# Query products of two tiles at a time in quarters of TensorE's array, normalized into SBUF, with fewer PSUM banks for the attention

## The chip, the cores and the metric

The kernel runs on one core of a Trainium2 chip. The metric is the device time of one execution in microseconds. All data are float32.

## The reference

The kernel fuses a linear attention with a feed-forward layer. What is computed:

```python
kv  = np.einsum('bhsd,bhse->bhde', k, v)          # 8 batches, 8 heads, 576 positions, 64 wide
out = np.einsum('bhsd,bhde->bhse', q, kv)
rms = np.sqrt(np.mean(out * out, axis=-1, keepdims=True) + 1e-06)
out = out / rms * g_norm                          # per head
x   = out.transpose(0, 2, 1, 3).reshape(4608, 512)
h   = x @ w_in                                    # 512 -> 2048
r   = np.maximum(h, 0.0)
y   = (r * r) @ w_out                             # 2048 -> 512
```

In the attention each head's keys-values matrix `kv` is 64 by 64, and each query row is multiplied by the matrix of its own head.

## The kernel before

The 4608 rows are cut into 36 tiles of 128 rows, and four tiles make a strip. Nine strips pass through the feed-forward layer one after the other. Up and down projections of most strips are done with a scheme of seven products instead of eight (Strassen's kind): `up` runs products 1, 2, 6, 5, 7, 3, 4 (`ORDER`) for each of four column groups, and `down` or `down_deep` does the same for the way down. The products accumulate in four PSUM banks called `ps_A` (two buffers), `ps_B` and `ps_C`. ScalarE copies some of them to SBUF (`snap`, L573), VectorE adds others and applies the squared relu (L622, L623). A product of `up` is eight records on TensorE, "a step" below.

The attention of the next strip is cut into small pieces (`slices`) that `attend` puts between the steps of the strip at hand, so the attention's matmuls stand in TensorE's queue among those of the feed-forward layer. Their order is written out by hand; no planner moves them. All engines take their instructions in the order in which they were recorded. The pieces, for batch `b` and pair of heads `p`:

- `transposed_query` (L320): queries transposed so that two heads of 64 lie on 128 partitions. For the first two batches TensorE does it, through PSUM; later VectorE does.
- `key_value` (L344): ten matmuls, each giving 64 rows of output from 64 columns, so that the two heads stand side by side in the two column halves of the array. ScalarE copies the two 64 by 64 results onto the diagonal of a 128 by 128 matrix `kvd`, whose other half is zero (L353, L354).
- `query(n)` (L411): `products_x` multiplies one tile's transposed queries by `kvd`, four matmuls of 128 by 128 by 128 (L380). Every ninth tile, made of the remaining 64 rows of two batches, takes eight matmuls with 64 columns of weights (L375). Then ScalarE squares the tile (L386), VectorE sums by head (L388), and after a square root and a Newton step (L389 to L400) VectorE multiplies by the inverse norm (L407). For later tiles this product is written back into the PSUM bank.
- `features` (L454, on TensorE, tiles 4 to 8) or `squares_x` (L462, for tiles 9 to 35: VectorE transposes blocks of 32 by 32, a DMA on SP's queue writes to DRAM, and four more read back) lay the tile out as the feed-forward layer's input `xT`.

The first four tiles have code of their own (`first_queries`, `first_normalized`, `first_features`), used in the first 30 us.

All PSUM tiles of the attention share four banks of the pool `apsum`, under the tag `at`. With the four of the feed-forward layer these are all eight.

Of the kernel before, what the change touches and what calls it, by code (L numbers as in the profile page):

```python
# [10 lines left out]
FP32 = mybir.dt.float32  # L11
# [3 lines left out]
AF = mybir.ActivationFunctionType  # L15
ALU = mybir.AluOpType
AX = mybir.AxisListType
# [3 lines left out]
def kernel(  # L21
# [34 lines left out]
    nc = tc.nc  # L56
    P = 128
    B, H, S, D = q.shape
    n_tok = B * S
    d_model = H * D  # L60
    d_ff = moe_w_in.shape[1]
    NP = H // 2
    FC = d_ff // P
    C = S // P
    REST = S - C * P
    PAIR = 2 * C + 1
    assert 2 * REST == P
    N_TILE = n_tok // P
    NT = 4
# [6 lines left out]
    X_ON_PE = 2  # L76
# [3 lines left out]
    qkv_pool = ctx.enter_context(tc.tile_pool(name="qkv", bufs=2))  # L80
    rest_pool = ctx.enter_context(tc.tile_pool(name="rest", bufs=1))
    qt_pool = ctx.enter_context(tc.tile_pool(name="qt", bufs=NP + 1))
    xn_pool = ctx.enter_context(tc.tile_pool(name="xn", bufs=2))
    xt_pool = ctx.enter_context(tc.tile_pool(name="xt", bufs=2))
    small = ctx.enter_context(tc.tile_pool(name="small", bufs=3))
    g_pool = ctx.enter_context(tc.tile_pool(name="g", bufs=4))
# [1 line left out]
    conv = ExitStack()  # L88
    raw_pool = conv.enter_context(tc.tile_pool(name="raw", bufs=8))
    wtmp = conv.enter_context(tc.tile_pool(name="wtmp", bufs=4))  # L90
    apsum = ctx.enter_context(tc.tile_pool(name="apsum", bufs=4, space=bass.MemoryType.PSUM))
    fpsum = ctx.enter_context(tc.tile_pool(name="fpsum", bufs=1, space=bass.MemoryType.PSUM))
    ctx.enter_context(tc.manual_schedule())

# [68 lines left out]
    def load_next(q_eng=nc.sync):  # L163
        u = next(to_load, None)
        if u is not None:
            load(*u, q_eng)
# [144 lines left out]
    qT, kvd, x_n, xt = {}, {}, {}, {}  # L311
    flat = lambda t: t.rearrange("p h d -> p (h d)")

    def open_rest(b):
        t = qt_pool.tile([P, NP, P], FP32, name="qT_rest", tag="qT_rest", bufs=1)
        for p in range(NP):
            qT["rest", b // 2, p] = t[:, p]
        return t

    def transposed_query(b, p):  # L320
        t = main.pop(("q", b, p))
        if b >= Q_ON_PE:
            qT[b, p] = qt_pool.tile([P, C, P], FP32, name="qT", tag="qT")
            nc.vector.transpose(out=flat(qT[b, p]), in_=flat(t))
            if b % 2 and p == NP - 1:
                nc.vector.transpose(
                    out=open_rest(b).rearrange("p q (k t) -> p q k t", k=4),
                    in_=squares(q_rest[b // 2]).rearrange("p k q f -> p q k f"),
                )
            return  # L330
        ps = apsum.tile([P, C, P], FP32, name="t_ps", tag="at")
        for c in range(C):
            nc.tensor.transpose(ps[:, c, :], flat(t[:, c]), ident)
        qT[b, p] = qt_pool.tile([P, C, P], FP32, name="qT", tag="qT")
        nc.scalar.copy(qT[b, p], ps)
        if b % 2:
            t = q_rest[b // 2][:, 2 * p : 2 * p + 2]
            ps = apsum.tile([P, P], FP32, name="tr_ps", tag="at")
            nc.tensor.transpose(ps, flat(t), ident)
            if p == 0:  # L340
                open_rest(b)
            nc.scalar.copy(qT["rest", b // 2, p], ps)

    def key_value(b, p):  # L344
        tk, tv = main.pop(("k", b, p)), main.pop(("v", b, p))

        ps = apsum.tile([P, D], FP32, name="kv_ps", tag="at")
        for c in range(C + 1):
            for h in range(2):
                a, w = (tk[:, h, c, :], tv[:, h, c, :]) if c < C else (k_rest[:, 2 * p + h], v_rest[:, b % 2, 2 * p + h])  # L350
                nc.tensor.matmul(ps[ts(h, D)], lhsT=a, rhs=w, start=c == 0, stop=c == C)  # L351
        d = kv_all[:, (NP * b + p) % (2 * NP + 1)]
        nc.scalar.copy(d[0:D, 0:D], ps[0:D])  # L353
        nc.scalar.copy(d[D:P, D:P], ps[D:P])  # L354
        kvd[b, p] = d
        if b < 2:
            if b == 1 and p < 2:
                load_next()
        else:
            load_next()  # L360
            if p == NP - 1 and b + 1 < B:
                load_rest(b + 1, nc.sync)
                load_q_rest(b + 1, nc.sync)

    by_head = lambda t: t.rearrange("p (h d) -> p h d", d=D)

    def products_x(n):
        m, c = divmod(n, PAIR)
        ps = apsum.tile([P, d_model], FP32, name="x_ps", tag="at")
        for p in range(NP):  # L370
            o = ps[:, ts(p, P)]
            if c == C:
                for h in range(2):
                    half = slice(REST * h, REST * (h + 1))
                    nc.tensor.matmul(  # L375
                        o[half], lhsT=qT["rest", m, p][:, half], rhs=kvd[2 * m + h, p], start=True, stop=True
                    )
            else:
                b, c_b = (2 * m, c) if c < C else (2 * m + 1, c - C - 1)
                nc.tensor.matmul(o, lhsT=qT[b, p][:, c_b, :], rhs=kvd[b, p], start=True, stop=True)  # L380
        return ps

    def mean_squares(ps):
        n = ps.shape[-1] // D
        sq = xn_pool.tile([P, d_model], FP32, name="sq", tag="sq", bufs=1)
        nc.scalar.activation(sq, ps, AF.Square)  # L386
        ms = small.tile([P, H], FP32, name="ms", tag="ms")
        nc.vector.reduce_sum(out=ms, in_=by_head(sq), axis=AX.X)  # L388
        nc.vector.tensor_scalar(out=ms, in0=ms, scalar1=1.0 / D, scalar2=EPS, op0=ALU.mult, op1=ALU.add)  # L389
        return ms  # L390

    def inverse_root(ms):
        r = small.tile([P, H], FP32, name="rms", tag="rms")
        nc.scalar.activation(r, ms, AF.Sqrt)
        nc.vector.reciprocal(r, r)

        t = small.tile([P, H], FP32, name="newton", tag="newton")
        nc.vector.scalar_tensor_tensor(out=t, in0=ms, scalar=-0.5, in1=r, op0=ALU.mult, op1=ALU.mult)
        nc.vector.tensor_tensor(out=t, in0=t, in1=r, op=ALU.mult)
        nc.vector.scalar_tensor_tensor(out=r, in0=t, scalar=1.5, in1=r, op0=ALU.add, op1=ALU.mult)  # L400
        return r

    def normalized(n, ps, r):

        on_pe = n < X_ON_PE * C + (X_ON_PE > 1)
        x_n[n] = xn_pool.tile([P, d_model], FP32, name="x_n", tag="x_n") if on_pe else ps
        nc.vector.tensor_tensor(  # L407
            out=by_head(x_n[n]), in0=by_head(ps), in1=r.unsqueeze(2).to_broadcast([P, H, D]), op=ALU.mult
        )

    def query(n):  # L411
        ps = products_x(n)
        normalized(n, ps, inverse_root(mean_squares(ps)))

    first = {}

    def first_queries(p):
        ps = apsum.tile([P, NT, P], FP32, name="x_ps", tag="at")  # L420
        for n in range(NT):
            nc.tensor.matmul(ps[:, n, :], lhsT=qT[0, p][:, n, :], rhs=kvd[0, p], start=True, stop=True)
        first[p] = flat(ps), mean_squares(flat(ps))

    def first_normalized(p):
        ps, ms = first.pop(p)
        x_n["first", p] = t = xn_pool.tile([P, NT, P], FP32, name="x_n", tag="x_n")
        r = inverse_root(ms)
        nc.vector.tensor_tensor(
            out=by_head(flat(t)), in0=by_head(ps), in1=r.unsqueeze(2).to_broadcast([P, H, D]), op=ALU.mult  # L430
        )
# [9 lines left out]

    def first_features(p):
        t, x = x_n.pop(("first", p)), open_xt(0)
        ps = apsum.tile([P, NT, P], FP32, name="xt_ps", tag="at")
        for n in range(NT):
            nc.tensor.transpose(ps[:, n, :], t[:, n, :], ident)
        nc.scalar.activation(x[:, :, p, :], flat(ps).rearrange("p (a t) -> p a t", t=SQ), AF.Copy, scale=g_col)

    def open_xt(s):
        if s not in xt:  # L450
            xt[s] = xt_pool.tile([P, STRIP // SQ, NP, SQ], FP32, name="xT", tag="xT")
        return xt[s]
# [40 lines left out]
    slices, ready = [], {}  # L493
# [10 lines left out]
    for b in range(1, B):  # L504
        for p in range(NP):
            slices += [(transposed_query, (b, p)), (key_value, (b, p))]
        first_n = b // 2 * PAIR + (C if b % 2 else 0)
        ns = list(range(first_n, first_n + C + b % 2))
        for i in range(len(ns) + 1):
            if i < len(ns):  # L510
                slices.append((query, (ns[i],)))
            if 0 < i <= len(ns):
                slices.append((features if b < X_ON_PE else squares_x, (ns[i - 1],)))
            if i > 0 and ns[i - 1] % NT == NT - 1:
                ready[ns[i - 1] // NT] = len(slices)
    slice_at = [0]

    def attend(n):
# [216 lines left out]
    place = lambda s, p: LAST_PLACE if s == N_STRIP - 1 and p in (5, 3) else PLACE  # L735
# [170 lines left out]
```

## Time and profile before

| What | Value |
|---|---|
| Median of 7 runs | 949.74 us (948.86 to 954.33) |
| The profiled execution | 950.99 us, its span 949.2 us |
| TensorE matmuls busy | 923.0 us, 97% |
| TensorE weight loads busy | 817.6 us, 86% |
| VectorE busy | 671.1 us, 71% |
| ScalarE busy | 231.2 us, 24% |
| DMA, mean over the span | 196 GB/s |
| Granted TensorE clock | 0.998 |

The profile counts a float32 matmul of the products as two records, each with its own weight load: the 112 matmuls of L380 are 224 records. A record lasts longer than the distance to the next one, because matmuls overlap in the array. What a matmul costs is therefore read from the distance between starts in the timeline and not from its mean duration.

### The profile page before, as it was taken

How to read it: one execution, taken by the hardware profiler on the slowest of the kernel's cores; microseconds unless marked ns; L12 is line 12 of the kernel's file. 1: busy time of each engine (PE TensorE's matmuls, PEld its weight loads, DVE VectorE, ACT ScalarE, POOL GpSimd, SP SyncE). 2: the span in 40 equal slices, each digit the busy share in tenths (PEclk: the TensorE clock that was granted, in tenths of full speed). 3: DMA queues.
4: the chain of work that ended last, by engine and by line, in shares of the span. 5: the costliest groups of instructions: out<-in, count | busy, mean ns of one | idle time of the engine just before them, and what ended most of it. 6: DMA issues, size and time to landing. Idle time of an engine off the chain costs nothing.

```text
span 949.2 us, 15646 instructions
## 1 busy us (share of the span) xinstructions
PE 923.0 (97%) x6144; PEld 817.6 (86%) x6144; DVE 671.1 (71%) x1217; ACT 231.2 (24%) x508; POOL 1.7 (0%) x7
## 2 busy tenths in 40 slices
PE   4899999999999999999999999999999999999998
PEld 3444888888888998899989998999889988998898
DVE  3998864585447995589648974798569854983396
ACT  3797441320023102210222012201220022002200
POOL 0000000000000000000000000000000000000000
PEclk9999999999999999999999999999999999999999
DMA  8799884536984586548663875387516821692075
GB/s 249 254 298 294 268 231 144 123 113 225 314 245 121 202 299 187 118 159 308 210 146 99 307 248 135 92 292 244 170 29 244 286 88 63 213 310 70 0 254 179
DMA packets 164281, 185.85 MB, mean 196 GB/s; under 512 B 83952, under 2 KB 137712, under 8 KB 155632
## 3 DMA queue, kind: packets, MB, share of 16 engines
q1 hardware_dynamic: 163888, 184.72, 61.6%
q8 instruction: 48, 0.79, 0.3%
q10 hardware_dynamic: 320, 0.13, 0.1%
q14 instruction: 25, 0.20, 0.1%
HBM read 153.62 MB, written 31.20 MB: 195 GB/s over the span
## 4 chain that ended last, share of the span: by engine, by line
PE 90%; DVE 4%; DMA 4%; ACT 1%; issue 1%; SPq 0%; DVEq 0%; ACTq 0%
PE ps_A L563 29%; PE ps_B L748 18%; PE ps_A L748 14%; PE ps_B L563 14%; PE ps_C L563 7%; PE x_ps L380 3%; PE kv_ps L351 2%; DMA raw<-in_moe_w_out_dram 2%; PE ps_A L599 1%; DMA w_blk<-w_out 1%; PE ps_B L599 1%; DVE w_c L222 1%; DMA q_rest<-in_q_dram 1%; DMA q<-in_q_dram 0%; PE x_ps L375 0%
## 5 line engine op out<-in xcount | busy, mean ns | idle before, releaser
L563 PE MATMUL ps_A<-x_t,w_in 128*128 128x256 f32 x768 | 182.6, 381 | 1.3 <-DVE gt L622 1.3
L563 PEld LDWEIGHTS ps_A<-x_t,w_in 128*128 128x128 f32 x768 | 143.6, 190 | 21.1 <-DVE gt L622 2.1
L748 PE MATMUL ps_B<-w_blk,g_s 128*128 128x128 f32 x896 | 109.2, 275 | 0.0
L748 PEld LDWEIGHTS ps_B<-w_blk,g_s 128*128 128x128 f32 x896 | 104.6, 192 | 0.0
L748 PE MATMUL ps_B<-w_blk,gt 128*128 128x128 f32 x672 | 84.2, 275 | 0.0
L748 PE MATMUL ps_A<-w_blk,g_s 128*128 128x128 f32 x672 | 81.9, 275 | 0.0
L748 PEld LDWEIGHTS ps_B<-w_blk,gt 128*128 128x128 f32 x672 | 80.1, 192 | 0.4
L748 PEld LDWEIGHTS ps_A<-w_blk,g_s 128*128 128x128 f32 x672 | 78.4, 192 | 0.0
L622 DVE TENSOR_TENSOR gt<-ps_C,snap 128x512 f32<-128x512 f32 x32 | 22.1, 690 | 66.8 <-PE ps_C L563 66.7
L623 DVE SCALAR_TENSOR_TENSOR gt<-gt 128x512 f32<-128x512 f32 x96 | 66.5, 692 | 3.3
L573 ACT COPY snap<-ps_A 128x512 f32<-128x512 f32 x68 | 39.8, 586 | 113.7 <-PE ps_A L563 101.3
L622 DVE TENSOR_TENSOR gt<-ps_A,snap 128x512 f32<-128x512 f32 x32 | 22.0, 688 | 61.6 <-PE ps_A L563 61.5
L748 PE MATMUL ps_A<-w_blk,gt 128*128 128x128 f32 x504 | 63.1, 275 | 0.0
L563 PE MATMUL ps_A<-xT,w_in 128*128 128x256 f32 x256 | 61.2, 382 | 0.0
L563 PE MATMUL ps_C<-xT,w_in 128*128 128x256 f32 x256 | 61.0, 381 | 0.0
L242 DVE TENSOR_TENSOR gt<-gt 128x2048 f32<-128x2048 f32 (+1 forms) x31 | 58.1, 1874 | 4.0 <-PE ps_C L563 3.8
L563 PE MATMUL ps_B<-x_t,w_in 128*128 128x256 f32 x256 | 60.9, 381 | 0.0
L563 PE MATMUL ps_B<-xT,w_in 128*128 128x256 f32 x256 | 60.7, 380 | 0.0
L748 PEld LDWEIGHTS ps_A<-w_blk,gt 128*128 128x128 f32 x504 | 59.7, 192 | 0.0
L388 DVE TENSOR_REDUCE ms<-sq 128x8 f32<-128x512 f32 x36 | 24.6, 684 | 44.9 <-ACT sq L386 44.2
L563 PEld LDWEIGHTS ps_C<-xT,w_in 128*128 128x128 f32 x256 | 48.1, 190 | 6.8 <-issue 0.2
L563 PEld LDWEIGHTS ps_B<-xT,w_in 128*128 128x128 f32 x256 | 48.3, 190 | 6.5
(117 smaller groups left out, 1236.0 us busy)
## 6 DMA issues: line engine op xcount, KB each, us to landing
w_blk<-w_deep SPq DMA_DIRECT2D x49, 1024.0 KB, 5.5
w_blk<-w_out SPq DMA_DIRECT2D x49, 768.0 KB, 5.2
w_blk<-w_out SPq DMA_DIRECT2D x11, 1024.0 KB, 6.5
raw<-in_moe_w_in_dram SPq DMA_DIRECT2D x16, 512.0 KB, 6.4
raw<-in_moe_w_out_dram SPq DMA_DIRECT2D x16, 512.0 KB, 6.2
k<-in_k_dram SPq DMA_DIRECT2D x30, 256.0 KB, 2.9
v<-in_v_dram SPq DMA_DIRECT2D x30, 256.0 KB, 3.3
w_deep<-w_t SPq DMA_DIRECT2D x7, 1024.0 KB, 8.6
```

Source lines behind the costliest of these rows:

```text
L222: yield nc.vector.scalar_tensor_tensor(out=ci, in0=high, scalar=-(2**30), in1=ci, op0=ALU.bitwise_and, op1=ALU.bitwise_or)
L242: eng.tensor_tensor(out=out, in0=a, in1=b, op=ALU.subtract)
L351: nc.tensor.matmul(ps[ts(h, D)], lhsT=a, rhs=w, start=c == 0, stop=c == C)
L380: nc.tensor.matmul(o, lhsT=qT[b, p][:, c_b, :], rhs=kvd[b, p], start=True, stop=True)
L388: nc.vector.reduce_sum(out=ms, in_=by_head(sq), axis=AX.X)
L563: nc.tensor.matmul(bank[BANK[p]][:, i, :], lhsT=lhsT(k), rhs=rhs(k), start=p in (1, 5, 2) and i == 0 and k == 0, stop=k == n - 1, skip_gro ...
L573: nc.scalar.copy(snap[p], b)
L599: nc.tensor.matmul(ps, lhsT=w_in[:, kc % KH, g, kc // KH * 2 + fh, ts(i, P)], rhs=xt[0][:, :, kc, :], start=kc == 0, stop=kc == NP - 1,)
L622: nc.vector.tensor_tensor(out=o, in0=b, in1=a, op=ALU.add)
L623: nc.vector.scalar_tensor_tensor(out=o, in0=o, scalar=0.0, in1=o, op0=ALU.max, op1=ALU.mult)
L748: nc.tensor.matmul(chain[c][x][:, i, :], lhsT=a[:, f, :], rhs=w[:, f, :], start=p not in (6, 7, 3) and j in ((1, 2) if place(s, p) is LAST ...
```

## The change

`products_x` now takes one or two tiles. Each matmul of 128 by 128 by 128 becomes four of 64 by 64 by 64: the contraction is cut by head (`row`, the two row halves of the array), and the output rows by 64 (`half`, the two column halves). The zero halves of `kvd` are no longer read. The two row halves write to different PSUM banks: the output is one tile of two banks, with the tag `x` and one buffer, indexed by row half, then tile, then column. The ninth tiles are done in the same way and may share a call with their neighbour.

The tiles of a batch are taken by twos: (query, query, normalize, features or squares for each). A batch with an odd number has five tiles, hence two pairs and a single; one with an even number has four, hence two pairs. Batches 1 to 7 make 14 pairs and 4 singles. `query` holds the matmuls, the squares and the sums, and `normalized`, a piece of its own, holds the square root, the Newton step (now once for both tiles) and the multiplication. This writes to SBUF (`x_n`) for all tiles, and puts the heads back in order on the way. The pool `xn` has three buffers shared by `sq`, `x_n` and `x_q`; before it had two and one for `sq` alone.

`apsum` keeps two banks for `at`. The transposed queries of batches 0 and 1 use the two-bank tile `x`; the transposes of the remaining rows use the free columns of the bank that the keys-values product will use. The first four tiles use the banks `A`, `B` and `C` of the feed-forward layer, which is not running yet.

```diff
-    xn_pool = ctx.enter_context(tc.tile_pool(name="xn", bufs=2))
+    xn_pool = ctx.enter_context(tc.tile_pool(name="xn", bufs=3))
...
-    apsum = ctx.enter_context(tc.tile_pool(name="apsum", bufs=4, space=bass.MemoryType.PSUM))
+    apsum = ctx.enter_context(tc.tile_pool(name="apsum", bufs=2, space=bass.MemoryType.PSUM))
...
-        ps = apsum.tile([P, C, P], FP32, name="t_ps", tag="at")
+        ps = apsum.tile([P, 2, C, P], FP32, name="t_ps", tag="x", bufs=1)[:, 0]
...
-            ps = apsum.tile([P, P], FP32, name="tr_ps", tag="at")
+            kv_places[b, p] = apsum.tile([P, 2 * P], FP32, name="kv_ps", tag="at")
+            ps = kv_places[b, p][:, P : 2 * P]
...
-        ps = apsum.tile([P, D], FP32, name="kv_ps", tag="at")
+        place = kv_places.pop((b, p), None) or apsum.tile([P, 2 * P], FP32, name="kv_ps", tag="at")
+        ps = place[:, 0:D]
...
-    def products_x(n):
-        m, c = divmod(n, PAIR)
-        ps = apsum.tile([P, d_model], FP32, name="x_ps", tag="at")
+    def products_x(ns):
+
+        ps = apsum.tile([P, 2, 2, d_model // 2], FP32, name="x_ps", tag="x", bufs=1)
         for p in range(NP):
-            o = ps[:, ts(p, P)]
-            if c == C:
+            for i, n in enumerate(ns):
+                m, c = divmod(n, PAIR)
                 for h in range(2):
                     half = slice(REST * h, REST * (h + 1))
...
-                b, c_b = (2 * m, c) if c < C else (2 * m + 1, c - C - 1)
-                nc.tensor.matmul(o, lhsT=qT[b, p][:, c_b, :], rhs=kvd[b, p], start=True, stop=True)
+                    if c == C:
+                        q, b = qT["rest", m, p], 2 * m + h
+                    else:
+                        b, c_b = (2 * m, c) if c < C else (2 * m + 1, c - C - 1)
+                        q = qT[b, p][:, c_b]
+                    for r in range(2):
+                        row = slice(D * r, D * (r + 1))
+                        nc.tensor.matmul(
+                            ps[half, r, i, ts(p, D)], lhsT=q[row, half], rhs=kvd[b, p][row, row], start=True, stop=True
+                        )
         return ps
...
+    def mean_squares(parts):
+        ms = small.tile([P, 2, H], FP32, name="ms", tag="ms")[:, : len(parts)]
+        for i, ps in enumerate(parts):
+            sq = xn_pool.tile(list(ps.shape), FP32, name="sq", tag="x_n")
+            nc.scalar.activation(sq, ps, AF.Square)
...
+    def query(ns):
+        ps = products_x(ns)
+        parts = [ps[:, :, i] for i in range(len(ns))]
+        queried.append((parts, mean_squares(parts)))
+
+    def normalized(ns):
+        parts, ms = queried.pop()
+        r = inverse_root(ms)
+        for i, n in enumerate(ns):
+            x_n[n] = xn_pool.tile([P, d_model], FP32, name="x_n", tag="x_n")
+            o = x_n[n].rearrange("p (q r d) -> p r q d", r=2, d=D)
+            x = parts[i].rearrange("p r (q d) -> p r q d", d=D)
+            w = r[:, i].rearrange("p (r q) -> p r q", r=2).unsqueeze(3).to_broadcast([P, 2, NP, D])
+            nc.vector.tensor_tensor(out=o, in0=x, in1=w, op=ALU.mult)
...
-        ps = apsum.tile([P, NT, P], FP32, name="x_ps", tag="at")
+        ps = fpsum.tile([P, NT, P], FP32, name="x_ps", tag="A", bufs=2)
...
-        ps = apsum.tile([P, NT, P], FP32, name="xt_ps", tag="at")
+        ps = fpsum.tile([P, NT, P], FP32, name="xt_ps", tag="BC"[p % 2])
...
-        for i in range(len(ns) + 1):
-            if i < len(ns):
-                slices.append((query, (ns[i],)))
-            if 0 < i <= len(ns):
-                slices.append((features if b < X_ON_PE else squares_x, (ns[i - 1],)))
-            if i > 0 and ns[i - 1] % NT == NT - 1:
-                ready[ns[i - 1] // NT] = len(slices)
+        for i in range(0, len(ns), 2):
+            slices += [(query, (ns[i : i + 2],)), (normalized, (ns[i : i + 2],))]
+            for n in ns[i : i + 2]:
+                slices.append((features if b < X_ON_PE else squares_x, (n,)))
+                if n % NT == NT - 1:
+                    ready[n // NT] = len(slices)
```

More of the change, by code (lines that the diff above doesn't have):

```diff
@@ L318, in open_rest @@
         return t
+    kv_places = {}
     def transposed_query(b, p):
@@ L365 @@
     by_head = lambda t: t.rearrange("p (h d) -> p h d", d=D)
-    def products_x(n):
-        m, c = divmod(n, PAIR)
-        ps = apsum.tile([P, d_model], FP32, name="x_ps", tag="at")
+    def products_x(ns):
+        ps = apsum.tile([P, 2, 2, d_model // 2], FP32, name="x_ps", tag="x", bufs=1)
         for p in range(NP):
-            o = ps[:, ts(p, P)]
-            if c == C:
+            for i, n in enumerate(ns):
+                m, c = divmod(n, PAIR)
                 for h in range(2):
                     half = slice(REST * h, REST * (h + 1))
[L375 to L378, printed above, removed]
-                b, c_b = (2 * m, c) if c < C else (2 * m + 1, c - C - 1)
-                nc.tensor.matmul(o, lhsT=qT[b, p][:, c_b, :], rhs=kvd[b, p], start=True, stop=True)
-        return ps
[L383 to L388, printed above, removed]
+                    if c == C:
[8 more added lines that the diff above has]
+                        )
+        return ps
+    def mean_squares(parts):
[3 more added lines that the diff above has]
+            nc.scalar.activation(sq, ps, AF.Square)
+            if len(ps.shape) == 3:
+                sq = sq.rearrange("p r e -> p (r e)")
+            nc.vector.reduce_sum(out=ms[:, i], in_=by_head(sq), axis=AX.X)
         nc.vector.tensor_scalar(out=ms, in0=ms, scalar1=1.0 / D, scalar2=EPS, op0=ALU.mult, op1=ALU.add)
@@ L392, in inverse_root @@
     def inverse_root(ms):
-        r = small.tile([P, H], FP32, name="rms", tag="rms")
+        r, t = (small.tile([P, 2, H], FP32, name=n, tag=n)[:, : ms.shape[1]] for n in ("rms", "newton"))
         nc.scalar.activation(r, ms, AF.Sqrt)
         nc.vector.reciprocal(r, r)
-        t = small.tile([P, H], FP32, name="newton", tag="newton")
         nc.vector.scalar_tensor_tensor(out=t, in0=ms, scalar=-0.5, in1=r, op0=ALU.mult, op1=ALU.mult)
@@ L401, in inverse_root @@
         return r
[L403 to L413, printed above, removed]
+    queried = []
+    def query(ns):
[11 more added lines that the diff above has]
+            nc.vector.tensor_tensor(out=o, in0=x, in1=w, op=ALU.mult)
     first = {}
     def first_queries(p):
-        ps = apsum.tile([P, NT, P], FP32, name="x_ps", tag="at")
+        ps = fpsum.tile([P, NT, P], FP32, name="x_ps", tag="A", bufs=2)
         for n in range(NT):
             nc.tensor.matmul(ps[:, n, :], lhsT=qT[0, p][:, n, :], rhs=kvd[0, p], start=True, stop=True)
-        first[p] = flat(ps), mean_squares(flat(ps))
+        first[p] = flat(ps), mean_squares([flat(ps)])
     def first_normalized(p):
@@ L427, in first_normalized @@
         x_n["first", p] = t = xn_pool.tile([P, NT, P], FP32, name="x_n", tag="x_n")
-        r = inverse_root(ms)
+        r = inverse_root(ms)[:, 0]
         nc.vector.tensor_tensor(
```

## The prediction

> **What bounds the kernel now.** I read the page first, its busy times and the row of slices, then the groups of instructions kept apart by shape, then the timeline of TensorE where query products stand.
>
> ```profile
> PE 923.0 (97%) x6144; PEld 817.6 (86%) x6144; DVE 671.1 (71%) x1217; ACT 231.2 (24%) x508; POOL 1.7 (0%) x7
> PE   4899999999999999999999999999999999999998
> PEclk9999999999999999999999999999999999999999
> ```
>
> TensorE (PE) is full from about 75 us to the end, at full clock. Every microsecond taken out of its queue after about 100 us should shorten the span, as long as nothing else is late. All query products but those of the first four tiles lie there:
>
> ```profile
> L380 PE MATMUL x_ps<-kv_all,qT 128*128 128x128 f32 x224 | 29.5, 275 | 0.0
> L375 PE MATMUL x_ps<-kv_all,qT_rest 128*64 128x128 f32 x64 | 4.8, 280 | 0.9 <-ACT kv_all L354 0.9
> L351 PE MATMUL kv_ps<-v,k 128*64 128x64 f32 x480 | 21.4, 234 | 0.0
> L388 DVE TENSOR_REDUCE ms<-sq 128x8 f32<-128x512 f32 x36 | 24.6, 684 | 44.9 <-ACT sq L386 44.2
> L407 DVE TENSOR_TENSOR x_ps<-x_ps,rms 128x512 f32<-128x512 f32 x27 | 18.9, 700 | 3.2 <-DVE rms L400 0.5
> ```
>
> L380 waits for nothing: what it costs is its length. The price is the distance between starts (first column, us):
>
> ```profile
> 501.84 1.89 PE L563 MATMUL ps_C<-xT,w_in 128*128 128x256 f32 x8
> 503.56 1.05 PE L380 MATMUL x_ps<-kv_all,qT 128*128 128x128 f32 x8
> 504.45 1.89 PE L563 MATMUL ps_A<-x_t,w_in 128*128 128x256 f32 x8
> 506.18 1.89 PE L563 MATMUL ps_B<-x_t,w_in 128*128 128x256 f32 x8
> ```
>
> A step of `up` takes 506.18 - 504.45 = 1.73 us, and a tile of L380 takes 504.45 - 503.56 = 0.89 us. Now a stretch with both kinds of half-array work:
>
> ```profile
> 688.62 0.81 PE L563 MATMUL ps_A<-x_t,w_in 128*128 128x256 f32 x3
> 689.37 0.69 PE L351 MATMUL kv_ps<-v,k 128*64 128x64 f32 x16
> 689.88 0.29 PE L351 MATMUL kv_ps<-v_rest,k_rest 128*64 128x64 f32 x4
> 690.10 1.99 PE L563 MATMUL ps_B<-x_t,w_in 128*128 128x256 f32 x8
> 691.93 1.89 PE L563 MATMUL ps_A<-x_t,w_in 128*128 128x256 f32 x8
> ...
> 696.21 1.99 PE L563 MATMUL ps_A<-x_t,w_in 128*128 128x256 f32 x8
> 698.13 1.09 PE L375 MATMUL x_ps<-kv_all,qT_rest 128*64 128x128 f32 x16
> 699.15 1.99 PE L563 MATMUL ps_A<-xT,w_in 128*128 128x256 f32 x8
> 700.99 0.38 PE L563 MATMUL ps_C<-xT,w_in 128*128 128x256 f32 x1
> ```
>
> The sixteen records of L351 start within 0.51 us, though each lasts 222 ns. Record by record in the same trace they start in twos, one for each column half, 7 ns apart, and a new two follows every 58.4 ns. **So the halves of the array do work side by side.** Entering and leaving this mode costs: three L563 records (0.216 each) from 688.62 end at 689.27, but L351 starts at 689.37 (0.10); its first two stand 0.05 longer than the later ones; the last is followed by L563 0.09 late; and the next step takes 1.83 instead of 1.73 (0.10). Together 0.34 us a block.
>
> **PE: what goes.** 28 tiles of L380 at 0.893 us: 25.0. Four tiles of L375: a start 0.09 late (1.92 after the step before, where a step behind keys-values takes 1.83), 1.02 long, next step 0.11 longer: 1.22 each, 4.9. Sum 29.9 us.
>
> **PE: what comes.** A tile is 16 matmuls of 64 by 64 by 64, 32 records, four to a set with one in each quarter. If all four run side by side as the two of L351 do, a set takes 58.4 ns: the stream is as long (64 columns) and so is the weight load. A pair is 16 sets, 0.93, and with the change of mode 1.28 us; a single is 0.47 + 0.34 = 0.81. 14 x 1.28 + 4 x 0.81 = 21.2 us. **Gain 8.7 us.** The changed order of instructions has 18 such blocks, each between two whole steps, so the change of mode is paid once for each.
>
> No row of before shows work in two row halves, so the set's time is the uncertain term. From below it is 58.4 ns (one stream's own time). From above it is twice that, if row halves take turns (a pair then 2.21 us). I take the lower end: the nearest row is L351, which differs only in its rows.
>
> **A rule against it.** The Trainium skill's page "TensorE: Matmul & The Clock Gate", section "Back-to-back issue gap", gives about 60 cycles (some 25 ns) as the least distance between starts for 1 to 64 columns. By it four records cost 100 ns and not 58.4, a pair 1.95 and all blocks 14 x 1.95 + 4 x 1.15 = 31.9 us: an estimate of 2 us lost. The row says otherwise for different tiles of the array: 7 ns between the two of L351, hence four in about 28 ns, below 58.4. I take the row. But L351 has only 20 records, which may have been queued ahead; a pair has 64. Semaphore records of PE's sequencer show how fast it fills the queue: at 12.75, 12.89 and 13.01 us it passed four matmuls each in about 0.13 us with the semaphore's own 0.05, some 20 ns a matmul, and a quarter matmul (two records) is needed only every 29 ns. So supply should hold.
>
> **Waits and the other engines.** ScalarE's squares and VectorE's sums, multiplications and block transposes stay, one each a tile at the same sizes (0.60, 0.68, 0.70, 0.71 us). The small operations L389 to L400 (0.17 + 0.21 + 0.20 + 3 x 0.17) are issued 18 times for 32 tiles: VectorE loses about 14 x 0.87 = 12 us, of 671, off the path. Five DMAs a tile stay, in the same order on SP's queue; a pair's two follow each other within two steps. Loads of q, k, v keep their place, since `key_value` issues them. The weights' stream belongs to the way down, where later strips have no query products.
>
> New waits:
>
> - A pair must find the one two-bank buffer free, that is, both multiplications of the pair before done. This chain is 0.3 + 2 x 0.60 + 0.68 + 0.17 + 0.24 + 0.24 + 0.6 + 2 x 0.70 = 4.8 us, and up to 2 more behind a step's L622, L623 and snap. In the changed order the nearest two blocks of `up` have five steps between them, 8.6 us. Covered; without that cover it would cost about 1 us at three places.
> - Behind the sums VectorE holds the L622 and L623 of later steps. Product 4 needs product 7's L622, one step apart. In the order VectorE gets this L622 before the multiplications, or the block stands after it. I count nothing; each failure would cost about 1 us.
> - A multiplication may have to wait for an `x_q` store in the buffer that it reuses; those stores are at least four steps old (7 us). Nothing.
> - Tile 8, the single of batch 1: its transposes on PE (`features`) now stand two steps behind its products; before they stood some thirty us behind. PE gets there after 3.46 us. VectorE does L622 and L623 of product 2 (1.4), the sum by about 1.8, waits for ScalarE, whose square root stands behind product 6's snap (1.73 + 0.3 + 0.59 = 2.6), then 0.25 + 0.24 + 0.6 + 0.70: 4.5. **PE waits 1.0 us, once.** Tiles 4 to 7 have 16-record blocks between (3.46 us each, two of them) and are in time.
> - Two `at` banks instead of four: keys-values blocks stand two or more steps apart and ScalarE's two copies take 0.41. Nothing. In the first 30 us TensorE waits for DMA and copies; the new banks (A, B, C) are read before their next use. Taken as 0, bounds -0.5 to +1.
>
> Sum: 949.2 - 8.7 + 1.0 = 941.5 us of span, or 943.2 for the profiled run (950.99). The median shown is 1.25 below that run, hence **942.0 us**.
>
> **Rivals.**
>
> 1. *The row halves take turns* (at the weight load or at the PSUM write, which now goes to two banks of the same partitions). For it: no row of before uses row halves. Against it: column halves share partitions on the input side and still run together. Then 14 x 2.21 + 4 x 1.28 = 36.1 us against 29.9, with the wait +7.2: **956.9, slower**. The point from which it decides: 18 x 0.34 + 256 sets x T = 28.9 us, so T above 89 ns a set loses.
> 2. *The quarters overlap in part, or the change of mode is dearer*: 75 ns a set (+4.2), or 0.25 us more a block (+4.5). For it: four weight loads at once are not shown. Against: L375 and L351 have the same overheads. **946.4**.
> 3. *The gain is given back in waits*: chained pieces put two squares and two sums before VectorE's next L622, and the one buffer stalls a few pairs, some 4 us. For it: VectorE already waits 44 us for the squares. Against: the order above. **946**.
>
> **How the numbers follow.** Forecast 0.75, rival 1 0.14, rival 2 0.07, rival 3 0.04. This kernel's runs tell a change from none at about 0.3%, 2.8 us: faster means below 946.9, slower above 952.6. Rivals 2 and 3 lie at the edge. Faster 0.78, same 0.08, slower 0.14. The forecast's own range is 938 (no wait at tile 8, mode change half as dear) to 945. The stated range, 938 to 955, takes in rivals 2 and 3 and the lower half of rival 1's spread.
>
> **What would show it.** In the changed profile the query products should have 1024 records of 64 by 64, a pair's block should last about 0.93 us between its first start and the 64th and delay the next step to 1.28 after its own natural start. If the block lasts 1.9, rival 1 holds. The transposes of tile 8 should show about 1 us waiting for VectorE. No new wait above 1 us should stand before L563. I would be wrong if sets come every 89 ns or more, or if TensorE's idle time grows by over 5 us.

## The result and the profile after

The changed kernel's median is 947.35 us (944.23 to 949.18, 13 runs) against 951.05 us for the kernel before on the same chip (32 runs). The ratio is 0.9959, with a 95% interval of 0.9948 to 0.9970. The change is a gain of 3.7 us by the medians and of 3.9 by the ratio, and the interval lies wholly below one. The forecast was 942.0, which is 7.7 below the 949.74 known then; the direction came true, and about half of the size. The profiled execution took 946.87 us, with a span of 945.1 us, 4.1 less than before.

The page's first rows, which answer to those shown of before:

```profile
PE 915.4 (97%) x6880; PEld 805.2 (85%) x6880; DVE 658.2 (70%) x1147; ACT 226.9 (24%) x494; POOL 1.7 (0%) x7
...
PE   4789999999999999999999999999999999999998
...
PEclk9999999999999999999999999999999999999999
```

VectorE fell by 12.9 us, where about 12 were foretold, which shortens nothing by itself, since VectorE isn't the bound. TensorE's row says more: its third slice (47 to 71 us) went from 9 to 8. That is before the first query product of the changed kind.

The query products are now line L386. The list of the tile `x_ps` gives their count, their least, median and longest duration in ns, and the first and last start:

```profile
L386 PE MATMUL x_ps<-kv_all,qT x896: 218/218/267, 103.1 to 787.2; 64*64 64x64 f32 x180
...
L386 PE MATMUL x_ps<-kv_all,qT_rest x128: 218/218/267, 102.9 to 698.1; 64*64 64x64 f32 x128
```

These are the 1024 records foretold. The timeline shows one pair between two whole steps of `up` (start, busy time, operation, count):

```profile
496.05 1.89 PE L576 MATMUL ps_B<-xT,w_in 128*128 128x256 f32 x8
497.87 0.34 PE L386 MATMUL x_ps<-kv_all,qT_rest 64*64 64x64 f32 x8
498.04 0.30 PE L386 MATMUL x_ps<-kv_all,qT 64*64 64x64 f32 x8
...
498.74 0.30 PE L386 MATMUL x_ps<-kv_all,qT 64*64 64x64 f32 x8
498.96 1.99 PE L576 MATMUL ps_A<-x_t,w_in 128*128 128x256 f32 x8
500.80 0.38 PE L576 MATMUL ps_A<-xT,w_in 128*128 128x256 f32 x1
```

From one step's start to that of the step after next is 500.80 - 496.05 = 4.75 us. Two plain steps take 2 x 1.73, so the pair with its change of mode costs 1.29. The forecast had 1.28. The 64 records start within 0.94 us: four starts 6 to 7 ns apart, and a new four every 58.4 ns. The quarters do run side by side, and the change of mode costs what it cost keys-values. Taken from step to step in the same way, the 14 pairs cost 1.29 and the 4 singles 0.82 each: 21.3 us, where 21.2 were forecast.

So the gain of 8.7 us exists, and over half of it was lost elsewhere. The view of TensorE's waits between 60 and 300 us lists tile, line and releaser, then the total, the number and the longest in us. After the change it reads:

```profile
PE kv_ps L355 <- ACT qT_rest L345: 3.4, 2, 3.1
PE ps_A L576 <- DMA w_blk<-w_out: 1.7, 1, 1.7
PE xt_ps L473 <- DVE x_n L427: 1.1, 1, 1.1
PE ps_A L576 <- ACT snap L586: 0.7, 1, 0.7
PE kv_ps L355 <- DMA v<-in_v_dram: 0.6, 1, 0.6
PE ps_B L576 <- DMA w_blk<-w_out: 0.3, 1, 0.3
```

Before, the same stretch held four waits (`kv_all` holds the keys-values matrices):

```profile
PE t_ps L333 <- DMA q<-in_q_dram: 1.1, 1, 1.1
PE x_ps L375 <- ACT kv_all L354: 0.9, 1, 0.9
PE ps_A L563 <- ACT snap L573: 0.7, 1, 0.7
PE ps_A L563 <- DMA w_blk<-w_out: 0.5, 1, 0.5
```

The `kv_ps` wait on ScalarE is new. Its place on TensorE's timeline, where the bracket is the wait ahead of the row:

```profile
64.69 0.28 PE L342 MATMUL kv_ps<-ident,q_rest 128*128 128x128 f32 x1
64.81 3.60 PE L612 MATMUL ps_B<-xT,w_in 128*128 128x512 f32 x8
71.53 0.88 PE L355 MATMUL kv_ps<-v,k 128*64 128x64 f32 x16 [3.12 <-ACT qT_rest L345]
72.19 0.43 PE L355 MATMUL kv_ps<-v_rest,k_rest 128*64 128x64 f32 x4
72.56 5.04 PE L612 MATMUL ps_A<-xT,w_in 128*128 128x512 f32 x8
77.43 0.60 PE L335 MATMUL t_ps<-ident,q 128*128 128x128 f32 x4
```

And ScalarE's timeline in the same run:

```profile
70.74 0.57 ACT L337 COPY qT<-t_ps 128x512 f32<-128x512 f32 x1
71.21 0.27 ACT L345 COPY qT_rest<-kv_ps 128x128 f32<-128x128 f32 x1
```

The transpose of the remaining queries (L342) was done by about 65 us. ScalarE reached its copy at 71.21, since it still converted weights for the way down (L204, L207) and applied squares and relus of earlier steps (L619, L620). Before the change this copy was as late, but the keys-values product had a bank of its own and was done before it:

```profile
68.27 0.69 PE L351 MATMUL kv_ps<-v,k 128*64 128x64 f32 x16
...
71.07 0.27 ACT L342 COPY qT_rest<-tr_ps 128x128 f32<-128x128 f32 x1
```

Now the product is a later writer of the tile `kv_ps` that the copy reads. The idle time had a second price: from 71.9 us the granted clock was 0.5 for 3.4 us, and the step at L612 took 5.04 us instead of 3.60.

An account of the 4.1 us of span, from the two traces:

| Term | us |
|---|---|
| 18 blocks in quarters | -8.7 |
| first 256-column step starts at 99.26 instead of 95.54 (the wait on L345 and its slow clock, less the wait on `q` that it covers) | +3.7 |
| transposes of tile 8 | +1.1 |
| `w_blk` on strip 1's way down: 2.0 instead of 0.5 | +1.5 |
| a load of `v` at strip 2's start | +0.6 |
| wait for `kv_all` before the first block, gone | -0.9 |
| two late waits of 0.64 on VectorE's L622, gone | -1.3 |
| sum | -4.0 |

The first row is the forecast's calculation, confirmed by the steps above and by an experiment below; the others are read from the traces. The load of `v` took only 3.2 us; it was issued late, at 279.46, since it stands in SP's queue behind reads of `x_d` that had waited 10.1 us for their store (8.7 before).

### The profile page after: what moved, and what is told of

Its sections match the earlier page's. It is cut to its first block, busy times and chain, and to the rows that moved or that the text cites. A ratio compares the mean times of both kernels' runs of the same rounds, so it can differ in the third digit from the quotient of the medians.

```text
span 945.1 us, 17026 instructions
## 1 busy us (share of the span) xinstructions
PE 915.4 (97%) x6880; PEld 805.2 (85%) x6880; DVE 658.2 (70%) x1147; ACT 226.9 (24%) x494; POOL 1.7 (0%) x7
## 4 chain that ended last, share of the span: by engine, by line
PE 88%; DVE 4%; DMA 4%; ACT 2%; issue 1%; SPq 0%; DVEq 0%; ACTq 0%
PE ps_A L576 29%; PE ps_B L761 18%; PE ps_A L761 14%; PE ps_B L576 14%; PE ps_C L576 7%; PE kv_ps L355 2%; PE x_ps L386 2%; DMA raw<-in_moe_w_out_dram 1%; DVE w_c L222 1%; DMA x_d<-x_q 1%; DMA w_blk<-w_out 1%; DVE w_in L225 1%; DVE w_c L216 1%; PE ps_A L612 1%; DMA q<-in_q_dram 0%
## 5 line engine op out<-in xcount | busy, mean ns | idle before, releaser
L576 PEld LDWEIGHTS ps_B<-x_t,w_in 128*128 128x128 f32 x256 | 48.2, 190 | 6.7
```

Of the source, the lines that this page charges most:

```text
L576: nc.tensor.matmul(bank[BANK[p]][:, i, :], lhsT=lhsT(k), rhs=rhs(k), start=p in (1, 5, 2) and i == 0 and k == 0, stop=k == n - 1, skip_gro ...
```

## The experiments

Theory A said that the query blocks gained what was forecast, and that the shared bank and the transposes of tile 8 took half of it back. Theory B said that the quarters gained less. Below, "ratio" is the time over that of the kernel before on the same chip.

### e1: a bank of their own for the remaining queries

The two-bank tile `x` has room in its second bank:

```diff
-        ps = apsum.tile([P, 2, C, P], FP32, name="t_ps", tag="x", bufs=1)[:, 0]
+        both = apsum.tile([P, 2, C, P], FP32, name="t_ps", tag="x", bufs=1)
+        ps = both[:, 0]
...
-            kv_places[b, p] = apsum.tile([P, 2 * P], FP32, name="kv_ps", tag="at")
-            ps = kv_places[b, p][:, P : 2 * P]
+            ps = both[:, 1, 0]
```

> The changed kernel with one thing put apart: the transposes of the remaining rows of batch 1 go to the second bank of the two-bank tile x, which they leave free, and no longer to the bank in which the keys-values product accumulates. Theory (the shared bank makes the keys-values matmuls of batch 1 wait for ScalarE's copy): the 3.1 us wait before the first keys-values block at about 71 us, the smaller one at 98 us and the slow clock behind the first are gone; about 3.7 us under the changed kernel, ratio to before about 0.992, the first step of the first way down at about 95.5 us. Rival (the early loss comes from fewer banks or from the loads' timing): the wait goes, but the first step of the way down stays near 99 us and the ratio near 0.996.

A miss: 955.72 us against 951.58, ratio 1.0049 (1.0033 to 1.0064), slower than both kernels. TensorE's timeline shows why:

```profile
65.90 0.60 PE L336 MATMUL t_ps<-ident,q 128*128 128x128 f32 x4
72.15 0.47 PE L342 MATMUL t_ps<-ident,q_rest 128*128 128x128 f32 x1 [5.64 <-ACT qT L338]
72.42 6.42 PE L612 MATMUL ps_B<-xT,w_in 128*128 128x512 f32 x8
```

The copy of the first four transposes (L338) is recorded ahead of the fifth (L342), and both touch the tile `both`. The fifth writes the other bank, and it waits all the same: the dependence holds for the whole tile. The wait moved from the keys-values product to the transpose, with no step between that could hide it. It came four times (5.64 and three of about 1.7 us), and the clock was at half for 6.8 us. Hence the edit removed the sharing that was suspected and put a worse one in its place.

### e2: the shared bank alone

The kernel before, with nothing of the change but the shared `kv_ps` tile, and still four banks:

```diff
-            ps = apsum.tile([P, P], FP32, name="tr_ps", tag="at")
+            kv_places[b, p] = apsum.tile([P, 2 * P], FP32, name="kv_ps", tag="at")
+            ps = kv_places[b, p][:, P : 2 * P]
...
-        ps = apsum.tile([P, D], FP32, name="kv_ps", tag="at")
+        place = kv_places.pop((b, p), None) or apsum.tile([P, 2 * P], FP32, name="kv_ps", tag="at")
+        ps = place[:, 0:D]
```

> The kernel before, with the shared bank alone: the transposes of the remaining rows of batch 1 in the bank of the keys-values product, everything else as it was. Theory: keys-values waits about 3 us for ScalarE at about 71 us, the way down starts some 3.7 us later; slower than before by 3 to 4 us, ratio about 1.0035. Rival: no wait, or a wait that later slack takes up, ratio 1.000.

953.92 us, ratio 1.0028 (1.0017 to 1.0039): a loss of some 2.7 us by the ratio and 2.3 by the medians, a little under the 3 to 4 expected. The wait is back:

```profile
72.39 0.69 PE L355 MATMUL kv_ps<-v,k 128*64 128x64 f32 x16 [2.65 <-ACT qT_rest L345]
```

A second one of 0.34 comes later, and the clock was at half for 3.4 us. Since all four banks were there, it isn't their number that costs but what shares one.

### e3: the whole array again

e1 with pairs, one multiplication into SBUF and all else kept, but with products of 128 by 128:

```diff
-        ps = apsum.tile([P, 2, 2, d_model // 2], FP32, name="x_ps", tag="x", bufs=1)
+        ps = apsum.tile([P, 2, d_model], FP32, name="x_ps", tag="x", bufs=1)
...
+                o = ps[:, i, ts(p, P)]
...
+                    nc.tensor.matmul(o, lhsT=qT[b, p][:, c_b, :], rhs=kvd[b, p], start=True, stop=True)
```

> As e1_own_bank, but the products of the two tiles of a pair with the whole array, as in the kernel before (128 by 128 by 128, the ninth tiles in two column halves); pairs, banks and normalization into SBUF as in the change. Theory (the quarters save 8.7 us on TensorE): slower than e1_own_bank by 8 to 9 us, ratio to before about 1.000 to 1.001. Rival (part of the gain comes from pairing, the piece of its own for the normalization or the waits that they take away): it stays clearly faster than before, 0.997 or less.

963.93 us, ratio 1.0130 (1.0115 to 1.0144). The ratio to before missed, since its base e1 had become slower. What it was made for holds: 963.93 - 955.72 = 8.2 us are what the quarters alone bring, and theory B falls. From step to step, the 18 blocks take 30.3 us in e3's trace and 21.7 in e1's, a difference of 8.6.

### e4: the transposes of tile 8 later

e1, with `features` of tile 8 put behind the next keys-values product:

```diff
+            slices += [(features, (n,)) for n in held]
+            held.clear()
...
+                if n == X_ON_PE * C:
+                    held.append(n)
+                    continue
```

> As e1_own_bank, with the transposes of tile 8 put behind the next keys-values block, some three steps later. Theory (VectorE is late for them by 1.1 us and nobody else cares): the wait of 1.1 us at about 160 us goes, 1 us under e1_own_bank, ratio about 0.991. Rival (the microsecond is taken by the next late thing, the weights' load in the way down at about 250 us): no difference from e1_own_bank.

956.18 us, ratio 1.0046 (1.0028 to 1.0063). The wait at tile 8 is gone from the list, but the time is not clearly different from e1's. Inconclusive, because the runs of both kernels spread over more than 3 us.

### e5: both copies behind all transposes

e1 mended. All five transposes are recorded first, so none has a reader of its tile ahead of it:

```diff
+            nc.tensor.transpose(both[:, 0, c, :], flat(t[:, c]), ident)
...
+            nc.tensor.transpose(both[:, 1, 0], flat(q_rest[b // 2][:, 2 * p : 2 * p + 2]), ident)
...
+        nc.scalar.copy(qT[b, p], both[:, 0])
+        if b % 2:
+            nc.scalar.copy(qT["rest", b // 2, p], both[:, 1, 0])
```

> e1_own_bank mended: all five transposes of a pair of heads are recorded before ScalarE's two copies out of the tile x, so that none of them stands behind a copy. Theory (a reader of any part of a PSUM tile holds up every later writer of that tile, and ScalarE's copy is some 6 us late): no wait of keys-values and none of the transposes between 60 and 100 us, no slow clock there; about 3.7 us under the changed kernel, ratio to before about 0.992. Rival (the early stretch is bound by the weights' conversion, and the wait only showed it): TensorE waits elsewhere before 100 us, ratio 0.996 as the changed kernel.

946.61 us, ratio 0.9942 (0.9921 to 0.9963). The wait for ScalarE's copy and the slow clock are gone, and the first 256-column step starts at 95.84 us instead of 99.26. But the next in line show up in the list of TensorE's waits:

```profile
PE xt_ps L471 <- DVE x_n L425: 2.4, 2, 1.3
PE ps_A L574 <- DMA w_blk<-w_out: 2.1, 1, 2.1
PE t_ps L337 <- DMA q_rest<-in_q_dram: 1.4, 1, 1.4
```

With a start 3.4 us earlier the span is only 0.2 shorter. Of the 3.4 us, 1.0 is gone at the first block of query products, where a wait of 0.5 for `kv_all` is back, and 1.6 by the step behind the transposes at 110 us, which wait 1.3 us for VectorE; the late start of the change had covered both. The wait on `w_blk` grew by 0.4. The ratio lies between the two that were expected, 0.992 and 0.996. Its interval overlaps that of the change (0.9948 to 0.9970), so a gain of this edit over the change isn't shown.

### e6: both, and once more

e5 with e4's edit, run twice, on two chips.

> e5_copies_last with the transposes of tile 8 some three steps later, as in e4_later_features. Theory A (VectorE's lateness is paid in full): 1 us under e5_copies_last, 0.991. Theory B (the loads of the way down of strip 1 are the limit after it and take it back): the wait at about 160 us goes, the wait for w_blk at about 255 us grows by as much, no difference.

943.96 us, ratio 0.9919 (0.9899 to 0.9939). Of the two `xt_ps` waits that of tile 8 went, and the one at 110 us stayed. The time is 2.65 us under e5, where this expectation's theory A said 1, and the wait on `w_blk` did not grow (1.8 us in all), so its theory B is not borne out. The repeat, beside e9 below:

> e6_both a second time, beside the run above: 0.992 of before, within 0.002.

944.52 us, ratio 0.9946 (0.9933 to 0.9958). This lies just outside the 0.990 to 0.994 expected. The kernels are the same, and the medians differ by 0.6 us; the ratios differ mostly because the kernel before took 951.98 on one chip and 949.91 on the other. A fair figure lies between the two.

### e7: the same matmuls, quarter by quarter

e5 with the loops of `products_x` turned round, so that all matmuls of a quarter follow each other:

```diff
-        for p in range(NP):
-            for i, n in enumerate(ns):
-                for h in range(2):
-                    for r in range(2):
+        for h in range(2):
+            for r in range(2):
+                for p in range(NP):
+                    for i, n in enumerate(ns):
```

> e5_copies_last with the same small matmuls in another order: all pairs of heads and both tiles of one quarter of the array, then the next quarter. Theory (the gain is that neighbours in the queue sit in different quarters, and TensorE starts them in order): 64 records at 58.4 ns, 4.1 us a pair and 2.2 us a single instead of 1.28 and 0.81; some 45 us slower than e5_copies_last, near 987 us. Rival (the queue looks ahead and finds other quarters, or the small size itself is what pays): no more than a few us from e5_copies_last.

977.99 us, ratio 1.0274 (1.0241 to 1.0308), 31 us above e5 where some 45 were expected. The timeline of a pair:

```profile
513.87 0.32 PE L384 MATMUL x_ps<-kv_all,qT_rest 64*64 64x64 f32 x2
514.04 0.28 PE L384 MATMUL x_ps<-kv_all,qT 64*64 64x64 f32 x2
514.15 0.28 PE L384 MATMUL x_ps<-kv_all,qT_rest 64*64 64x64 f32 x2
...
514.62 0.33 PE L384 MATMUL x_ps<-kv_all,qT_rest 64*64 64x64 f32 x4
514.74 0.33 PE L384 MATMUL x_ps<-kv_all,qT 64*64 64x64 f32 x4
```

Two records take 0.117 us from start to start, 58 ns each: one after another, not four at once. The 64 records take 3.19 us instead of 0.94, and with the change of mode a pair costs 3.53, where 4.1 were expected: at a change of quarter (514.62) some records overlap. The size of the matmuls brings nothing by itself; neighbours in the queue must stand in different quarters.

### e8 and e9: what delays `w_blk`

On strip 1's way down the DMA engines were busy for 0.77 of the time before (206 to 258 us). The weight blocks stream in there beside strip 1's stores of its results. In the changed kernel the block waited for was issued at 245.09 us, 7.4 us before TensorE was ready for it (6.7 before the change), so it wasn't issued late. The view of the DMA issues ends with the us from issue to landing:

```profile
w_blk<-w_out SPq DMA_DIRECT2D x1, 1024.0 KB, 9.0
```

Before the change the same block took 6.4. e8 is e6 without those stores (`DEEP - 1` is strip 1), and so leaves that strip's rows out of the output:

```diff
     def send(s, th, eh, o):
+        if s == DEEP - 1:
+            return
```

> e6_both without the stores of strip 1's output rows, some 1 MB of the 13 MB that the way down of strip 1 moves; the rows of that strip are left out of the output. Theory (the wait for w_blk at about 255 us is DMA bandwidth): that wait of 1.7 us falls by half or more, 1 to 1.5 us under e6_both. Rival (the load is issued late, by a chain through VectorE's sums and their store): the wait stays.

940.37 us, ratio 0.9879 (0.9846 to 0.9912), from two runs. No wait on `w_blk` is left, and the block lands faster than in e6, where it took 8.8 us:

```profile
w_blk<-w_out SPq DMA_DIRECT2D x1, 1024.0 KB, 6.3
```

The medians lie 3.6 us apart, more than the 1.8 that waited there. In the traces e8 is 0.6 us ahead of e6 at 101 us, before the first of these stores, and gains 2.2 at the two waits on `w_blk`; the rest of the difference isn't explained, and e8 has only two runs. Before the change, the same stores did not slow the block. There the write of `w_deep` ahead of it had 1.3 us left at its issue, and in the change 2.6: with TensorE ahead the transfers crowd together. That this is why the stores now matter is argued, not tested. e9 keeps the stores and issues them behind the loads of strip 2 (`stream(4)`):

```diff
+    kept = []
+
+    def send(s, th, eh, o, now=False):
+        if s == DEEP - 1 and not now:
+            kept.append((s, th, eh, o))
+            return
...
                     stream(4)
+                    for x in kept:
+                        send(*x, now=True)
+                    kept.clear()
```

> e6_both with the stores of strip 1's output rows issued behind the loads for strip 2, some up to 40 us later; nothing is left out. Theory (bandwidth in the way down of strip 1): the wait for w_blk at about 251 us falls from 1.6 us to under 0.5, 1 to 2 us under e6_again, about 0.990 of before. Rival (the stores collide as much where they go now): the wait goes, and the loads of keys and values of strip 2 come late instead, no gain.

942.70 us, ratio 0.9918 (0.9904 to 0.9933). First e6 as repeated beside it, from the view of TensorE's waits:

```profile
PE ps_A L580 <- DMA w_blk<-w_out: 2.0, 1, 2.0
...
PE ps_B L580 <- DMA w_blk<-w_out: 0.5, 1, 0.5
```

In e9 the same view lists no `w_blk`, and the block landed after 6.5 us instead of 9.4. Its first row is another load:

```profile
PE kv_ps L353 <- DMA v<-in_v_dram: 1.6, 1, 1.6
```

So 2.5 us of waiting went and 1.6 came. More went with it: in e6's trace the clock was at half for 3.4 us from 251.8 us, a microsecond behind the end of the wait on `w_blk`, and in e9's it was not. e9's trace is of its slowest run (945.18 us), 3.7 us behind e6's at 104 us, where the edit changes nothing; from there to the start of strip 2 it gains 3.0. e9 has the lowest median of the complete kernels, 1.8 us below e6 beside it; the two intervals meet at 0.9933, so a gain over e6 is likely and not shown. Against the change itself, 0.9918 (to 0.9933) stands below 0.9959 (from 0.9948), so e9 beats both kernels, though it did not run beside the change.

## Why the prediction was partly right, and where it failed

- **The price of a block: right.** A set of four takes 58.4 ns and a pair 1.29 us (forecast 1.28). e3 finds 8.2 us for the quarters alone, where 8.7 was forecast. The failure lies in the waits.
- **The rule on the issue gap: rightly set aside.** By it a pair would have cost 1.95 us. Starts in different quarters stand 7 ns apart, and 64 in a row were supplied without a gap. Rival 1 (row halves take turns) and rival 2 (dearer overlap) fall by the same rows.
- **Tile 8: right.** One wait of 1.10 us on `x_n`, forecast 1.0. That tiles 4 to 7 are in time was luck in part: it held behind the late start, but e5 and e6 show 1.3 and 1.1 us of waiting for the first two of them.
- **The one buffer, L622 behind the sums, the `x_q` stores: right.** None appears among TensorE's waits. Two waits of 0.64 us on L622 even went. Rivals 2 and 3 named nearly the time that came, 946. For rival 2 this is chance. Rival 3 was right that the gain is given back in waits, but not the ones that it named.
- **The step that failed: "Two `at` banks instead of four: keys-values blocks stand two or more steps apart and ScalarE's two copies take 0.41. Nothing."** It took the copies by their length and the banks by their number. What counts is which instruction shares the tile with them. The remaining queries' transposes had moved into the tile of the keys-values product, which thus waits for ScalarE's copy; and the copy comes some 6 us after its transpose, because weight conversions, squares and relus stand ahead of it. The copy's time stood in the trace of before. In the runs this term measures +3.7 us of start, and 2.7 us of total when it is the only change (e2). Taking it out of the change again (e5) brought 0.7 us by the medians, not clear of noise, because other waits that the late start had covered came out.
- **The start of the kernel: also missed by "taken as 0, bounds -0.5 to +1".** This bound spoke of the first 30 us; the loss lies at 65 to 78 us, in the attention of batch 1, where no query product of the new kind stands. The sentence "No new wait above 1 us should stand before L563" named the right sign, and it was broken by the 3.12 us.
- **A term left out: "The weights' stream belongs to the way down, where later strips have no query products."** Being ahead on TensorE is worth nothing where a load lands last. On strip 1's way down the wait grew by 1.5 us; without the stores there (e8), or with them later (e9), it is gone. With the three mended, the bank, tile 8 and this, e9 stands at 0.9918, which is the forecast's own ratio (942.0 / 949.74); since the forecast counted a wait for tile 8 that e9 lacks, and had no waits on loads, that equality is chance.

Left open: whether e5 is faster than the change, which the intervals don't tell; how e6's remaining distance divides between loads of `v`, `q_rest` and `w_blk`, since each edit brought out the next; and the last microsecond between the medians of e6 and e8.

## What to carry to other kernels

When an output moves into a tile that another product also writes, look up when the reader of that output really runs, not how long it takes: a reader 6 us behind makes its tile's next writer wait, whichever bank or column it writes. Small matmuls pay only where neighbours in the queue stand in different quarters of the array. When TensorE becomes faster at the head of a kernel, expect loads to be next, and count a gain there only up to the next load that lands last.

## What the runs showed of the hardware

- Four quarters of the array worked at once: four 64 by 64 records start 6 to 7 ns apart and the next four 58.4 ns later, the same distance as between two halves. Queued quarter by quarter, the same 64 records took 3.19 us instead of 0.94. At a change of quarter the timeline shows groups of four instead of two (in e7 at 514.62 and 514.74), so only a few records overlap there.
- A stop of 3.1 us on TensorE went with 3.4 us at half clock, and one of 5.6 us with 6.8 us (e1). Against the kernel before, the work behind them stood 4.8 and 8.8 us later, about one and a half times the stop. On strip 1's way down a wait of 2.0 us went with 3.4 us at half clock (e6 as repeated), and waits of 1.7 (the change) and 2.1 us (e5) at the same place went with none; what decides between them no run here shows.
- The same 1 MB block of weights took 6.3 to 6.5 us from issue to landing without stores close to it (e8, e9) and 8.8 to 9.4 us with them (the change, e5, e6). Before the change it took 6.4 with them.
